# Block-sparse attention with a gated feed-forward layer: block numbers in one row, mask arithmetic on GpSimd, longer first K copies in the plan

## The chip, the cores and the metric

The kernel runs on one core of a Trainium2 chip. The metric is the device time of one execution in microseconds (us), given as the median of several runs. A core has TensorE (PE, with its weight loads shown as PEld), VectorE (DVE), ScalarE (ACT), GpSimd (POOL) and SyncE (SP); each takes its instructions in order, and they wait for each other through semaphores. Transfers are started by SP, ACT or POOL.

## What is computed

Attention over 4 batches, 8 heads, 768 positions of width 64, in blocks of 32 positions (24 blocks), and then a layer over the 3072 rows of 512 that come out. The mask lets a query block see its neighbours, the first and the last block, and three sampled blocks; the first and last query blocks see everything.

```python
scores = scale * np.matmul(q, k.transpose(0, 1, 3, 2))
mask = np.abs(blk_i - blk_j) <= window
mask = mask | (blk_i == 0) | (blk_j == 0) | (blk_i == n_blocks - 1) | (blk_j == n_blocks - 1)
for qb in range(n_blocks):
    for kb in sampled_blocks[qb]:
        mask[qb * block:(qb + 1) * block, kb * block:(kb + 1) * block] = True
attn = softmax(np.where(mask, scores, -1e9))
x = (attn @ v) as rows of 512
h = x @ w_in                                   # 512 -> 2048
out = (h / (1 + np.exp(-beta * h))) @ w_out    # 2048 -> 512
```

The block numbers `sampled_blocks` are 24 x 3 integers of 64 bits, known only at run time.

## The kernel before

Work is cut into tasks, each a short stretch of instructions of one engine. `add(name, engine, duration, emit, deps, prio, ...)` records a task with a planned duration. `Plan.run` (L51) then plays the tasks on the engines with those durations and priorities (smaller goes first), and its order is the order in which the instructions are written out. Where a task may run on two engines, the plan picks one by planned end times. So a changed planned duration changes the order on every engine and the engine of some tasks, and never the amount of work. `hw` and `dma` model a transfer, and `slack` delays a task after the tasks it depends on.

The attention goes by pairs of query blocks: 11 pairs in each of 4 batches, numbered n = 0 to 43. For each pair:

- `kg` (POOL, L560): reads six block numbers into registers and copies the six sampled K blocks from `KT` into a buffer `KG` (L566). `kn` (DVE or POOL, L569) adds the neighbour, first and last blocks.
- `sc` (PE, L653): first a matmul that writes the mask into the score bank (L658), then the scores from `KG` and `QT` (L668).
- `mx` (DVE, L679) row maxima, `ex` (ACT, L687) exponentials, `rc` (DVE, L693) reciprocals, `nrm` (POOL or DVE, L699) normalisation.
- `tp` (PE, L711) transposes, `ptv` (DVE, L715) their copy, `av` (PE, L727) the product with the gathered V blocks `VG`, `xv` (L735) its copy into `xT`.

`VG` comes by transfers from a V table in memory (SP, L627; tables written at L535), except the sampled V blocks of the first four pairs, which PE picks with 0/1 selection matrices (`pick`, L638). The first and last query blocks run as full rows (`gs` to `gx`, L754 to L827). The feed-forward layer runs in eight groups of rows: `h` (PE, L868), `tanh` (ACT, L874), `stt` (DVE, L879), `y` (PE, L896), output (ACT).

Ahead of all that stands the front, which the change touches:

- SP loads K, Q and V of batch 0 in halves of 768 KB (L433), ACT's queue loads the block numbers into `sbl` (`sbl`, L291: 72 single 4-byte words, the low halves of the 64-bit numbers) and then beta (L395).
- POOL turns the numbers into floats `sf` (L307) and into two tables of offsets (L309: `idx`), makes constants (`selc`, L364) and a half-precision row of block numbers (`srow`, L372).
- DVE computes the mask from `sf` in three tasks (`mask.0` to `mask.2`, L313 to L337): a sampled block that lies within the window, is the first or last block, or repeats an earlier one is masked out of its sampled place, since it is counted elsewhere. Each condition gives 0 or 1, joined by maximum, then scaled into a row `mrow`. PE spreads the row to 128 partitions (`maskb`, L342), DVE copies it into `maskr` (`maskc`, L345).
- PE makes the selection values from `srow` (`selb`, L379 and L381), ACT copies them (`selw`, L385), DVE compares them with the partition's position (`sel16`, L388).
- DVE casts K and Q of batch 0 to half precision (`cast`, L442), PE transposes them (`trK`, `trQ`, L508), ACT copies the transposes into `KT` and `QT` (`evK`, `evQ`, L259 and L265). DVE casts V (`vperm0`, L261).

The first gather needs `idx` and all four `evK`; the first `sc` needs `kg`, `kn`, `maskc` and all `evQ`.

Of the kernel before, what the change touches and what calls it, by code (L numbers as in the profile page):

```python
# [12 lines left out]
I32 = mybir.dt.int32  # L13
AF = mybir.ActivationFunctionType
ALU = mybir.AluOpType
# [3 lines left out]
NEG = -30000.0  # L19
# [16 lines left out]
class Plan:  # L36
# [9 lines left out]
    def add(self, *a, **k):  # L46
        t = Task(*a, **k)
        self.tasks.append(t)
        return t
# [133 lines left out]
def kernel(  # L183
# [11 lines left out]
    nc = tc.nc  # L195

    B, H, S, D = q.shape
    BLK = 32
    NB = S // BLK
# [15 lines left out]
    def sb(name, shape, dt=FP16):  # L215
        return pool.tile(shape, dt, name=name)
# [36 lines left out]
    add = plan.add  # L253
# [14 lines left out]
                out=out, in0=in_, scalar1=by, scalar2=1.0, op0=ALU.mult, op1=ALU.mult)  # L268


    sbl = sb("sbl", [1, NB, 3], I32)
    ctx_nc = nc

    def emit_ident():
# [2 lines left out]
    t_ident = add("ident", "POOL", 2.0, emit_ident, prio=-100)  # L277
# [3 lines left out]
    def emit_warm():  # L281
# [3 lines left out]
        out=warm[:, 0:1], in_=warm[:, 1:2], func=AF.Exp), deps=[t_warm0], prio=-150)  # L285

    def emit_sbl():
        src = sampled_blocks.tensor
        import dataclasses
        h = dataclasses.replace(src, shape=[NB, 6], dtype=I32)  # L290
        nc.scalar.dma_start(out=sbl, in_=bass.AP(tensor=h, offset=0, ap=[[0, 1], [6, NB], [2, 3]]))  # L291
    t_sbl = add("sbl", "ACT", 0.5, emit_sbl, prio=-200, dma=0.3, hw=1)

    sf = sb("sf", [1, NB - 2, 3], FP32)
    si = sb("si", [1, NB - 2, 3], FP32)
    sd = sb("sd", [1, NB - 2, 3], FP32)
    se = sb("se", [1, NB - 2, 3], FP32)
# [5 lines left out]
    t_iota = add("iota", "POOL", 0.6, emit_iota, prio=-99)  # L303

    def emit_idx():
        V = nc.gpsimd
        V.tensor_copy(out=sf, in_=sbl[:, 1:NB - 1, :])  # L307
        for t, m in ((offP, 16.0), (offV, 32.0)):
            V.tensor_scalar(out=t[:, :, 0:6], in0=sf[:, :, :].rearrange("o (p g) r -> o p (g r)", g=2),  # L309
                            scalar1=m, scalar2=1.0, op0=ALU.mult, op1=ALU.mult)  # L310
    t_idx = add("idx", "POOL", 0.6, emit_idx, deps=[t_sbl], prio=-99)

    def emit_mask0():  # L313
        V = nc.vector
        V.memset(sm5, 0.0)
        V.memset(sm5[:, 0:1, 3:4], 1.0)
        V.memset(sm5[:, NB - 3:NB - 2, 4:5], 1.0)
        V.tensor_tensor(out=sd, in0=sf, in1=si, op=ALU.subtract)
        V.tensor_tensor(out=sd, in0=sd, in1=sd, op=ALU.mult)
        V.tensor_scalar(out=sd, in0=sd, scalar1=1.5, scalar2=None, op0=ALU.is_lt)  # L320

    def emit_mask1():
        V = nc.vector
        V.tensor_scalar(out=se, in0=sf, scalar1=0.0, scalar2=None, op0=ALU.is_equal)
        V.tensor_tensor(out=sd, in0=sd, in1=se, op=ALU.max)
        V.tensor_scalar(out=se, in0=sf, scalar1=float(NB - 1), scalar2=None, op0=ALU.is_equal)
        V.tensor_tensor(out=sd, in0=sd, in1=se, op=ALU.max)
        V.tensor_tensor(out=se[:, :, 1:3], in0=sf[:, :, 1:3], in1=sf[:, :, 0:2], op=ALU.is_equal)

    def emit_mask2():  # L330
        V = nc.vector
        V.tensor_tensor(out=sd[:, :, 1:3], in0=sd[:, :, 1:3], in1=se[:, :, 1:3], op=ALU.max)
        V.tensor_tensor(out=se[:, :, 2:3], in0=sf[:, :, 2:3], in1=sf[:, :, 0:1], op=ALU.is_equal)
        V.tensor_tensor(out=sd[:, :, 2:3], in0=sd[:, :, 2:3], in1=se[:, :, 2:3], op=ALU.max)
        V.tensor_copy(out=sm5[:, :, 0:3], in_=sd)
        V.tensor_scalar(out=mrow, in0=sm5[:, :, :].rearrange("o a b -> o (a b)"),
                        scalar1=NEG / D, scalar2=None, op0=ALU.mult)  # L337
    t_mrow = None
    for part, f in enumerate((emit_mask0, emit_mask1, emit_mask2)):
        t_mrow = add(f"mask.{part}", "DVE", 0.95, f, deps=[t_idx, t_iota, t_ident, t_mrow], prio=-66.5)  # L340
    NM = (NB - 2) * 5
    t_mb = add("maskb", "PE", 0.3, lambda: nc.tensor.matmul(  # L342
        bank("mask")[:, 0:NM], lhsT=ones[0:1, :], rhs=mrow, start=True, stop=True),
        deps=[t_mrow], prio=-90, lat=0.2, opens=("mask",))
    t_mask = add("maskc", "DVE", 0.2, lambda: nc.vector.tensor_copy(  # L345
        out=maskr[:, :, :].rearrange("x a b -> x (a b)"), in_=bank("mask")[:, 0:NM]),
        deps=[t_mb], prio=-66, closes=("mask",))
# [16 lines left out]
    def emit_selc():  # L364
# [8 lines left out]
        out=srow, in_=sf[:, 0:2 * NSEL, :].rearrange("o a r -> o (a r)")), deps=[t_idx], prio=-98)  # L373
    t_selw = []
    for f in range(2):
        def emit_sb(f=f):
# [9 lines left out]
            out=sel16[:, f * SH:(f + 1) * SH], in_=bank(("selb", f))[:, 0:SH]),  # L386
            deps=[tb], prio=-88, closes=(("selb", f),)))
    t_sel = [add(f"sel16.{j}", "DVE", 0.27, lambda j=j: nc.vector.tensor_scalar(  # L388
        out=sel[j], in0=sel16, scalar1=pj[:, j:j + 1], scalar2=None, op0=ALU.is_equal),
        deps=t_selw, prio=-66.2) for j in range(J)]  # L390
# [5 lines left out]
        out=beta_row, in_=moe_beta.rearrange("(q x) -> q x", q=FQ)), prio=-140, dma=0.1, hw=1)  # L396
    t_id32 = add("id32", "DVE", 0.2, lambda: nc.vector.tensor_copy(
        out=ident32, in_=identity[0:4, 0:4]), deps=[t_ident], prio=-64)

    def emit_betaT():  # L400
        for i in range(4):
# [3 lines left out]
                  deps=[t_beta0, t_id32], prio=-55, lat=0.2, opens=("beta",))  # L405
    t_beta = add("betah", "DVE", 0.2, lambda: nc.vector.tensor_scalar(
        out=beta_sb[:, :].rearrange("x (q i) -> x i q", i=4),
        in0=bank("beta")[:, 0:N_FFC].rearrange("x (i q) -> x i q", i=4),
        scalar1=0.5, scalar2=None, op0=ALU.mult),
        deps=[t_betaT], prio=-55, closes=("beta",))  # L410
# [20 lines left out]
    for i, (nm, t, dst) in enumerate((("K", k, RK), ("Q", q, RQ), ("V", v, None))):  # L431
        for f in range(2):
            tl = add(f"ld{nm}0.{f}", "SP", 0.47, lambda i=i, t=t, f=f: nc.sync.dma_start(  # L433
                out=stage_half(i, f) if i < 2 else v_stage[:, f * HH:(f + 1) * HH, :],
                in_=src6(t, 0, f * HH, HH)), prio=-80 + i * 2 + f, dma=2.0, hw=1)
# [3 lines left out]
            for hp in range(2 * f, 2 * f + 2):  # L439
# [3 lines left out]
                        out=dst[:, 2 * hp:2 * hp + 2, :], in_=stage32(i, hp)),  # L443
                    deps=[tl], prio=-72 + 4 * i + hp)
# [13 lines left out]
    for c in range(4):  # L458
        for f in range(2):
            ps = slice(64 * f, 64 * f + 64)  # L460
            t_win.append(add(f"win{c}.{f}", "POOL", 0.6, lambda c=c, ps=ps: nc.gpsimd.dma_start(
                out=w_in_sb[ps, c, :], in_=w_in_r[c, ps, :]),
                deps=[tch], prio=-50 + 0.2 * c + 0.1 * f, dma=1.3, bulk=THR))
    for c in range(4):
        for f in range(2):
            ps = slice(64 * f, 64 * f + 64)
            t_wout.append(add(f"wout{c}.{f}", "POOL", 0.6, lambda c=c, ps=ps: nc.gpsimd.dma_start(
                out=w_out_sb[ps, 4 * c:4 * c + 4, :].rearrange("x i m -> x (i m)"), in_=w_out_r[c, ps, :]),
                deps=[tch], prio=-49 + 0.2 * c + 0.1 * f, dma=1.3, bulk=THR))
# [7 lines left out]
    for b in range(B):  # L477
        pr = prep_prio(b)
        if b:
            vperm[b] = []  # L480
            for nm, t, raw in (("V", v, RV), ("K", k, RK), ("Q", q, RQ)):
                tr = {"K": trK, "Q": trQ}.get(nm)
                for f in range(2):
# [4 lines left out]
                    else:  # L488
# [3 lines left out]
                             deps=free + [t_wout[-1]] if b == 1 else free,  # L492
                             prio=(-40 if b == 1 else pr - 30) + "VKQ".index(nm) + 0.5 * f, dma=2.55, bulk=THR)
# [8 lines left out]
        for nm, s16, dstT, tr, ev in (("K", RK, KT, trK, evK), ("Q", RQ, QT, trQ, evQ)):  # L502
            for hp in range(NHP):
                def emit_tr(nm=nm, s16=s16, b=b, hp=hp):
                    o = bank16((nm, b, hp))
                    for j in range(J):
                        for u in range(2):
# [5 lines left out]
                                prio=pr + hp, lat=0.2, opens=((nm, b, hp),))  # L513

                def emit_ev(eng, nm=nm, dstT=dstT, b=b, hp=hp):
# [4 lines left out]
                    else:  # L520
                        scale_on(eng, dst, src, SCALE)
                ev[b, hp] = add(f"ev{nm}{b}.{hp}", {"ACT": 0.71, "DVE": 0.86}, None, emit_ev,
                                deps=[tr[b, hp]], prio=pr + hp, closes=((nm, b, hp),))
# [3 lines left out]
        if b == 0:  # L527
            vperm[0], vtab[0] = [], []
            for f in range(2):
# [4 lines left out]
                    deps=[v0ld[f]], prio=-65))  # L534
                vtab[0].append(add(f"vtab0.{f}", "SP", 0.45, lambda cs=cs, vt_rows=vt_rows: nc.sync.dma_start(  # L535
                    out=vt_rows[:, :, cs], in_=Vn[0][:, :, cs]),
                    deps=[vperm[0][f]], prio=-64, dma=1.3, hw=1))
# [10 lines left out]
    for n, (b, p) in enumerate(order_pairs):  # L548
        pr = n * 10
# [37 lines left out]
                C(out=dst[:, 1, :, SN * w:(SN + 1) * w], in_=src[:, :, (NB - 1) * w:NB * w])  # L587
                C(out=dst[:, 1, :, (SN + 1) * w:(SN + 3) * w], in_=src[:, :, i0 * w:(i0 + 2) * w])
        kdeps = [evK[b, hp] for hp in range(NHP)] + ([sc[n - NKG]] if n >= NKG else [])
        kg[n] = add(f"kg{n}", "POOL", 1.15, emit_kg, deps=[t_idx] + kdeps, prio=pr)  # L590
        kn[n] = add(f"kn{n}", {"POOL": 0.5 + 0.6 * first_k, "DVE": 0.45 + 0.25 * first_k}, None,
                    emit_kn, deps=kdeps, prio=pr)

# [361 lines left out]
```

## Time and profile before

| what | value |
|---|---|
| three runs: median (range) | 316.14 us (315.14 to 317.6) |
| the profiled execution: time, span of its instructions | 316.81 us, 315.0 us |
| PE busy | 291.3 us, 92% of the span |
| DVE busy | 232.1 us, 74% |
| ACT busy | 212.4 us, 67% |
| POOL busy | 185.4 us, 59% |
| granted TensorE clock, mean | 0.978 |
| block numbers: issue on ACT's queue | 1.36 us from 0.74 |
| K of batch 0: first and second half landed | 4.8 us after an issue at 0.75; 6.8 us after one at 1.26 |
| first gather copy on POOL (L566) | 13.24 us |
| first pick on PE (L638) | 19.62 us |

All figures but the first line come from one profiled execution. Times in a timeline count from the start of the span. "Busy" is the time with an instruction in flight on an engine; an idle time is put down to the event that ended it. A PE that is busy need not be at its peak, since the granted clock can be lower and weight loads overlap.

### The profile page before, as it was taken

To read this page: it belongs to the slowest core of one execution; us is meant where nothing else is said; L and a number is where in the kernel's file an instruction comes from. 1 tells how busy PE (TensorE), PEld (TensorE's weight loads), DVE (VectorE), ACT (ScalarE), POOL (GpSimd) and SP (SyncE) were. 2 spreads that over 40 slices of the span, in tenths; PEclk is the share of its full clock that TensorE was granted. 3 is DMA by queue.
4 is the path that set the end of the run, shared out by engine and by line. 5 is a ranking of instruction groups with operands and counts; after the bars stand their busy time and mean duration, and the time that the engine had idled before them with its cause. 6 is when DMAs were issued, how large, how long until landed. Compare 5 with 4: busy or idle time off the path is not lost.

```text
span 315.0 us, 12633 instructions
## 1 busy us (share of the span) xinstructions
PE 291.3 (92%) x4569; PEld 179.8 (57%) x4569; DVE 232.1 (74%) x536; ACT 212.4 (67%) x625; POOL 185.4 (59%) x534
## 2 busy tenths in 40 slices
PE   0889869998989899999999999999999999999994
PEld 0645558756946676556556565545655555554671
DVE  2972785988899999999985478999679845670160
ACT  1753757875876989778785579857679835671361
POOL 3389985988388797599687354648836842200000
PEclk9999956999999999999999999999999999999999
DMA  7969999699976886345899752234233341100201
GB/s 248 354 138 209 218 212 194 125 202 248 204 152 133 250 151 137 109 129 100 151 171 242 175 152 77 67 115 109 83 90 90 84 138 49 35 1 33 100 2 67
DMA packets 41546, 43.70 MB, mean 139 GB/s; under 512 B 6152, under 2 KB 37000, under 8 KB 41484
## 3 DMA queue, kind: packets, MB, share of 16 engines
q1 hardware_dynamic: 27088, 25.32, 27.8%
q0 software_dynamic: 10784, 11.27, 24.1%
q10 hardware_dynamic: 3612, 6.30, 5.5%
q8 instruction: 36, 0.59, 0.8%
q14 instruction: 26, 0.21, 0.2%
HBM read 44.70 MB, written 9.44 MB: 172 GB/s over the span
## 4 chain that ended last, share of the span: by engine, by line
PE 68%; DMA 7%; DVE 7%; issue 5%; POOL 4%; SPq 3%; POOLq 1%; ACT 1%; DVEq 0%; ACTq 0%
PE bank L868 23%; PE bank L896 22%; PE bank L727 7%; PE bank L711 6%; DMA RQ<-in_q_dram 6%; PE bank L668 2%; SPq L627 2%; PE bank L658 2%; POOL KG L566 2%; PE bank L508 2%; DMA VG<-VT 1%; PE bank L638 1%; DVE SG L773 1%; POOLq L561 1%; DVE ST L679 1%
## 5 line engine op out<-in xcount | busy, mean ns | idle before, releaser
L699 POOL TENSOR_SCALAR PP<-PP,ST 128x256 f16<-128x256 f16 x176 | 83.5, 490 | 35.7 <-DVE ST L693 31.1
L868 PE MATMUL bank<-xT,w_in_sb 128*128 128x256 f16 (+1 forms) x512 | 94.9, 332 | 1.9 <-DVE g L879 1.3
L687 ACT ACTIVATE PP<-bank,ST 128x256 f16<-128x256 f32 x176 | 81.6, 485 | 17.5 <-DVE ST L679 14.3
L896 PE MATMUL bank<-w_out_sb,g 128*128 128x512 f16 x384 | 91.3, 380 | 0.8 <-DVE g L879 0.8
L874 ACT ACTIVATE t<-bank,beta_sb 128x512 f16<-128x512 f32 (+1 forms) x128 | 70.0, 595 | 18.6 <-PE bank L868 15.5
L879 DVE SCALAR_TENSOR_TENSOR g<-t,bank 128x512 f16<-128x512 f16 (+1 forms) x128 | 66.4, 547 | 19.6 <-ACT t L874 19.2
L566 POOL COPY KG<-KT 128x64 f32 x264 | 53.9, 253 | 34.1 <-PE bank L668 26.7
L868 PEld LDWEIGHTS <-w_in_sb 128*128 128x128 f16 x512 | 54.2, 115 | 26.5 <-issue 4.8
L679 DVE TENSOR_REDUCE ST<-bank 128x2 f32<-128x512 f32 x88 | 57.3, 680 | 10.7 <-PE bank L668 10.6
L896 PEld LDWEIGHTS <-g 128*128 128x128 f16 x384 | 34.7, 98 | 39.2 <-issue 4.5
L715 DVE COPY PT<-bank 128x1024 f16<-128x1024 f16 x44 | 30.2, 685 | 14.1 <-PE bank L711 13.6
L687 ACT ACTIVATION_READ_ACCUMULATOR PP<-bank,ST 128x1 f32 x176 | 38.2, 217 | 0.0
L727 PEld LDWEIGHTS <-VG 128*64 128x64 f16 x1408 | 27.4, 115 | 17.3 <-issue 13.1
L727 PE MATMUL bank<-PT,VG 128*64 128x32 f16 x1408 | 31.5, 186 | 4.3 <-issue 2.1
L265 ACT ACTIVATE osb<-bank 128x512 f32<-128x512 f32 x24 | 14.4, 599 | 22.8 <-PE bank L896 22.7
L711 PE MATMUL bank<-identity,PP 128*128 128x128 f16 x352 | 28.4, 225 | 0.5 <-DVE PTG L801 0.3
L711 PEld LDWEIGHTS <-PP 128*128 128x128 f16 x352 | 23.0, 100 | 7.6 <-POOL PP L699 0.9
L780 ACT ACTIVATE PG<-bank,SG 128x384 f16<-128x384 f32 x32 | 18.3, 578 | 5.2 <-DVE ST L693 2.3
L668 PE MATMUL bank<-KG,QT 64*32 64x256 f16 x704 | 18.8, 278 | 0.9 <-POOL KG L566 0.8
L791 POOL TENSOR_SCALAR PG<-PG,SG 128x768 f16<-128x768 f16 x14 | 13.2, 946 | 9.4 <-ACT PG L780 3.8
L259 ACT CAST xT<-bank 128x256 f16<-128x256 f32 x25 | 9.5, 381 | 12.8 <-PE bank L727 11.0
L773 DVE TENSOR_REDUCE SG<-bank 128x1 f32<-128x384 f32 x32 | 16.1, 546 | 0.6 <-PE bank L759 0.5
(94 smaller groups left out, 261.7 us busy)
## 6 DMA issues: line engine op xcount, KB each, us to landing
VG<-VT SPq DMA_DIRECT2D x244, 32.0 KB, 2.8
VG<-VT SPq DMA_DIRECT2D x40, 192.0 KB, 3.8
out_dram<-osb ACTq DMA_DIRECT2D x20, 256.0 KB, 2.2
RV<-in_v_dram POOLq DMA_DIRECT2D x6, 384.0 KB, 5.8
RK<-in_k_dram POOLq DMA_DIRECT2D x6, 384.0 KB, 6.3
RQ<-in_q_dram POOLq DMA_DIRECT2D x6, 384.0 KB, 6.0
VT<-Vn SPq DMA_DIRECT2D x3, 768.0 KB, 6.0
w_in_sb<-in_moe_w_in_dram POOLq DMA_DIRECT2D x8, 256.0 KB, 8.0
```

Source lines behind the costliest of these rows:

```text
L566: nc.gpsimd.tensor_copy(out=kg32[:, g, :, (SR + r) * W:(SR + r + 1) * W], in_=kt32[:, :, bass.ds(vals[3 * g + r], W)])
L668: nc.tensor.matmul(bk[u][hp * BLK:(hp + 1) * BLK, g * 256:(g + 1) * 256], lhsT=QT[b % 2][u * D:(u + 1) * D, hp, (i0 + g) * BLK:(i0 + g + 1 ...
L679: mx[n, u] = add(f"mx{n}.{u}", "DVE", 0.6, lambda n=n, u=u, sb_=sb_: nc.vector.tensor_reduce(out=sb_[:, 0, 2 * u:2 * u + 2], in_=bank(("S" ...
L687: nc.scalar.activation(out=pb[:, u, g, :], in_=bank(("S", n, u))[:, g * 256:(g + 1) * 256], func=AF.Exp, bias=sb_[:, 0, 2 * u + g:2 * u + ...
L699: (nc.vector if eng == "DVE" else nc.gpsimd).tensor_scalar(out=pb[:, u, g, :], in0=pb[:, u, g, :], scalar1=sb_[:, 2, 2 * u + g:2 * u + g + ...
L711: nc.tensor.transpose(out=o[:, s * P:(s + 1) * P], in_=pb[:, u, g, c * P:(c + 1) * P], identity=identity)
L715: ptv[n] = add(f"ptv{n}", "DVE", 0.61, lambda n=n: nc.vector.tensor_copy(out=PT[n % NPT], in_=bank16(("T", n))), deps=[tp[n]] + ([av[n - N ...
L727: nc.tensor.matmul(o[us, (g * NHP + hp) * BLK:(g * NHP + hp + 1) * BLK], lhsT=vgb[:, g, c, (2 * hp + u) * D:(2 * hp + u + 1) * D], rhs=pt[ ...
L868: nc.tensor.matmul(o[:, 0:TW], lhsT=w_in_v[:, c, f // 4, f % 4, :], rhs=xT[:, c, c0:c0 + TW], start=(c == 0), stop=(c == NHP - 1))
L874: lambda G=G, f=f, TW=TW, tt=tt: nc.scalar.activation(out=tt[:, 0:TW], in_=bank(("H", G, f))[:, 0:TW], func=AF.Tanh, bias=0.0, scale=beta_ ...
L879: lambda G=G, f=f, TW=TW, tt=tt, gg=gg: nc.vector.scalar_tensor_tensor(out=gg[:, f, 0:TW], in0=tt[:, 0:TW], scalar=1.0, in1=bank(("H", G, ...
L896: nc.tensor.matmul(o[:, :], lhsT=gg[:, f, s * P:(s + 1) * P], rhs=w_out_sb[:, f, :], start=(f == 0), stop=(f == N_FFC - 1))
```

## The change

Three edits. The block numbers are loaded whole, as one contiguous row of 144 words (`sbl` grows from 3 to 6 words per block), and the conversion to `sf` takes every second word. The mask tasks move from DVE to POOL: `mask.0` now holds only the three memsets and depends on nothing, `mask.1` and `mask.2` compute the conditions and join them by addition in place of maximum (a masked place then holds a count of 1 or more), with an equality between two rows written as a subtraction and a comparison with zero; they get priorities (-98.8, -97, -96) that put them before the first gather. The plan's duration of the gathers of pairs 0, 1 and 2 rises from 1.15 to 2.6, 2.6 and 1.6. The `slack` on `sbl` stands on a task that depends on none.

```diff
-    sbl = sb("sbl", [1, NB, 3], I32)
+    sbl = sb("sbl", [1, NB, 6], I32)
...
-        nc.scalar.dma_start(out=sbl, in_=bass.AP(tensor=h, offset=0, ap=[[0, 1], [6, NB], [2, 3]]))
-    t_sbl = add("sbl", "ACT", 0.5, emit_sbl, prio=-200, dma=0.3, hw=1)
+        nc.scalar.dma_start(out=sbl, in_=bass.AP(tensor=h, offset=0, ap=[[0, 1], [6, NB], [1, 6]]))
+    t_sbl = add("sbl", "ACT", 0.5, emit_sbl, prio=-200, dma=0.3, hw=1, slack=0.8)
...
-        V.tensor_copy(out=sf, in_=sbl[:, 1:NB - 1, :])
+        V.tensor_copy(out=sf, in_=sbl[:, 1:NB - 1, 0::2])
...
     def emit_mask0():
-        V = nc.vector
+        V = nc.gpsimd
         V.memset(sm5, 0.0)
         V.memset(sm5[:, 0:1, 3:4], 1.0)
         V.memset(sm5[:, NB - 3:NB - 2, 4:5], 1.0)
+
+    def emit_mask1():
+
+        V = nc.gpsimd
         V.tensor_tensor(out=sd, in0=sf, in1=si, op=ALU.subtract)
         V.tensor_tensor(out=sd, in0=sd, in1=sd, op=ALU.mult)
         V.tensor_scalar(out=sd, in0=sd, scalar1=1.5, scalar2=None, op0=ALU.is_lt)
-
-    def emit_mask1():
-        V = nc.vector
-        V.tensor_scalar(out=se, in0=sf, scalar1=0.0, scalar2=None, op0=ALU.is_equal)
-        V.tensor_tensor(out=sd, in0=sd, in1=se, op=ALU.max)
-        V.tensor_scalar(out=se, in0=sf, scalar1=float(NB - 1), scalar2=None, op0=ALU.is_equal)
-        V.tensor_tensor(out=sd, in0=sd, in1=se, op=ALU.max)
-        V.tensor_tensor(out=se[:, :, 1:3], in0=sf[:, :, 1:3], in1=sf[:, :, 0:2], op=ALU.is_equal)
+        for to in (0.0, float(NB - 1)):
+            V.tensor_scalar(out=se, in0=sf, scalar1=to, scalar2=None, op0=ALU.is_equal)
+            V.tensor_tensor(out=sd, in0=sd, in1=se, op=ALU.add)
 
     def emit_mask2():
-        V = nc.vector
-        V.tensor_tensor(out=sd[:, :, 1:3], in0=sd[:, :, 1:3], in1=se[:, :, 1:3], op=ALU.max)
-        V.tensor_tensor(out=se[:, :, 2:3], in0=sf[:, :, 2:3], in1=sf[:, :, 0:1], op=ALU.is_equal)
-        V.tensor_tensor(out=sd[:, :, 2:3], in0=sd[:, :, 2:3], in1=se[:, :, 2:3], op=ALU.max)
+        V = nc.gpsimd
+        for far in (1, 2):
+            V.tensor_tensor(out=se[:, :, far:3], in0=sf[:, :, far:3], in1=sf[:, :, 0:3 - far], op=ALU.subtract)
+            V.tensor_scalar(out=se[:, :, far:3], in0=se[:, :, far:3], scalar1=0.0, scalar2=None, op0=ALU.is_equal)
+            V.tensor_tensor(out=sd[:, :, far:3], in0=sd[:, :, far:3], in1=se[:, :, far:3], op=ALU.add)
         V.tensor_copy(out=sm5[:, :, 0:3], in_=sd)
         V.tensor_scalar(out=mrow, in0=sm5[:, :, :].rearrange("o a b -> o (a b)"),
-                        scalar1=NEG / D, scalar2=None, op0=ALU.mult)
-    t_mrow = None
-    for part, f in enumerate((emit_mask0, emit_mask1, emit_mask2)):
-        t_mrow = add(f"mask.{part}", "DVE", 0.95, f, deps=[t_idx, t_iota, t_ident, t_mrow], prio=-66.5)
+                        scalar1=NEG / D, scalar2=1.0, op0=ALU.mult, op1=ALU.mult)
+    t_m0 = add("mask.0", "POOL", 0.4, emit_mask0, prio=-98.8)
+    t_m1 = add("mask.1", "POOL", 0.9, emit_mask1, deps=[t_idx, t_iota], prio=-97)
+    t_mrow = add("mask.2", "POOL", 1.0, emit_mask2, deps=[t_m1, t_m0], prio=-96)
...
-        kg[n] = add(f"kg{n}", "POOL", 1.15, emit_kg, deps=[t_idx] + kdeps, prio=pr)
+        kg[n] = add(f"kg{n}", "POOL", 2.6 if n < 2 else 1.6 if n == 2 else 1.15, emit_kg, deps=[t_idx] + kdeps, prio=pr)
```

In the built program the front's order becomes: on POOL `idx`, `mask.0`, `selc`, `srow`, `mask.1`, `mask.2`, `kg0`, `kg1`; on DVE four K casts, three `sel16`, two Q casts, three `sel16`, `maskc`, two Q casts; on PE `trK0.0`, `selb0`, `selb1`, `trK0.1`, `maskb`, `trK0.2`, `trK0.3`; on ACT `evK0.0`, `selw0`, `selw1`, `evK0.1`. Before, `selb0`, `selb1` and `selw0`, `selw1` came first, and the mask tasks stood on DVE before the first cast and between the second and third.

## The prediction

> **What bounds the kernel now.** I read the page first, then busy time by stage, then the first 20 us instruction by instruction, because everything the diff edits lies there. By stage (stage, its length, busy time of PE, PEld, DVE, ACT, POOL, then granted clock, DMA share, GB/s):
>
> ```profile
> span 315.0 us, 12633 instructions
> PE 291.3 (92%) x4569; PEld 179.8 (57%) x4569; DVE 232.1 (74%) x536; ACT 212.4 (67%) x625; POOL 185.4 (59%) x534
> ...
> 0.00:19.60 19.60, 9.79 (x153) 6.99 (x153) 13.06 (x44) 8.92 (x15) 8.85 (x30) 1.00 0.78 262
> 19.60:36.60 17.00, 16.94 (x204) 9.26 (x196) 8.52 (x20) 8.86 (x32) 15.56 (x47) 1.00 1.07 202
> 36.60:52.40 15.80, 11.73 (x208) 9.01 (x207) 10.66 (x28) 10.30 (x42) 12.36 (x28) 0.57 1.05 213
> 52.40:80.00 27.60, 26.16 (x531) 19.05 (x531) 23.94 (x64) 20.86 (x66) 22.92 (x67) 1.00 0.94 189
> 80.00:120.00 40.00, 37.33 (x774) 28.11 (x770) 37.98 (x92) 33.56 (x102) 28.77 (x77) 1.00 0.83 178
> ```
>
> See that PE has no slack from 19.6 to 36.6 us (16.94 of 17.00): whatever moves the start of that stage moves all of it. PE is idle 9.8 us before it, 4.1 us in the next stage, 1.4 and 2.7 us in the two after. So the change is worth what it does to the moment when PE's first long run (the picks, L638) starts, plus what a new order does to 8.2 us of later idle time.
>
> The timeline of the front (start, length, instruction; in brackets the idle time before it and what ended it):
>
> ```profile
> 6.06 0.23 POOL L307 CAST sf<-sbl 1x66 f32<-1x66 int32 x1 [4.22 <-DMA sbl<-in_sampled_blocks_dram]
> ...
> 6.39 0.27 POOL L309 TENSOR_SCALAR offP<-sf 1x66 int32<-1x66 f32 x1
> ...
> 6.74 0.24 POOL L309 TENSOR_SCALAR offV<-sf 1x66 int32<-1x66 f32 x1
> ...
> 8.06 1.01 DVE L442 CAST RK<-g 128x768 f16<-128x768 f32 x2
> ...
> 10.59 0.27 PE L342 MATMUL bank<-mrow,ones 1*128 1x110 f16 x1
> 10.79 1.25 PEld L508 LDWEIGHTS <-RK 128*64 128x64 f16 x24
> ...
> 13.24 5.98 POOL L566 COPY KG<-KT 128x64 f32 x12 [5.49 <-ACT KT L259]
> ...
> 15.51 0.94 DVE L261 CAST Vn<-xT 128x1536 f16<-128x1536 f32 x1
> ```
>
> Block numbers reach POOL at 6.06. DVE then does mask arithmetic and casts the first K half only at 8.06, though that half landed 4.8 us after its issue at 0.75, so at 5.55 (next lines; the second K half at 8.05, the first Q half at 10.2). K's transposes, their copies on ACT and the first gather copies (13.24) follow from that.
>
> ```profile
> g<-in_k_dram SPq DMA_DIRECT2D x1, 768.0 KB, 4.8
> ...
> g<-in_k_dram SPq DMA_DIRECT2D x1, 768.0 KB, 6.8
> g<-in_q_dram SPq DMA_DIRECT2D x1, 768.0 KB, 8.4
> ```
>
> The line view of the gather copies, between 13 and 19.2 us, gives least, median and greatest duration in ns:
>
> ```profile
> L566 POOL COPY KG<-KT x12: 227/232/2580, 13.2 to 19.0; 128x64 f32 x12
> ```
>
> A copy of 0.23 us took 2.58 us. Its neighbours show when: it spans from 13.97 to 16.55, and DVE's Vn cast ends at 15.51 + 0.94 = 16.45. All that time DVE ran SBUF copies and casts back to back (two RQ casts, three KG copies, the Vn cast), and POOL did not get in between any two of them.
>
> **Part 1, the contiguous row.** Its issue took 1.36 us on ACT and POOL got the data at 6.06, after the first K half (5.55). The nearest short issue is beta's, 0.31 us; K's own first issue took 0.46. Bounds: POOL starts at about 2.9 if the row leaves before K's packets (an estimate: the DMA share is 0.07 up to 2 us and 0.93 from 2 to 4), or 5.5 if it still queues behind that half. I take 2.9, as a 0.31 us issue that starts with K's (0.74 and 0.75) ends first.
>
> **Part 2, the mask on POOL.** Removed from DVE: 13 small operations between 6.33 and 10.08, about 2.9 us, so the K casts can begin at 5.55. Added to POOL ahead of the first gather: 3 memsets and 15 operations on one partition, all but one dependent on the one before. A dependent pair on POOL starts 0.33 to 0.35 us apart (6.06, 6.39, 6.74); I take 0.35.
> - Row at 2.9; conversions, memsets, constants and the row's half copy start to start as now (1.5) plus 0.35 for the memsets plus 0.2: mask.1 starts at about 5.0. Two operations are through at 5.6.
> - DVE casts the first K half, 5.55 to 6.6 (1.01 us as at 8.06). Then POOL finishes mask.1, five operations, 1.6 us: 8.2.
> - At 8.05 the second K half lands. In the built order DVE now has, without a wait that lasts: two K casts (to 9.1), three selection compares of 0.33 (to 10.1; their input is ready at 8.9: one K transpose group of 0.75 from 6.1, then the 1.95 us that now lie between the first selection matmul and the end of the second ACT copy), two Q casts (to 11.2), three compares (to 12.3), then the mask's copy-out, which waits for PE. If POOL stays out as at 13.97, the eight operations of mask.2 run from 12.3 to 15.1 (8 x 0.35).
> - PE is in order, and the mask matmul (L342 before) stands between the second and third K transposes. Before it ran at 10.59 with no cost, and 2.65 us later the gathers began (13.24). Now it runs at 15.2, the gathers begin at 17.85: **4.6 us later**.
> - Part comes back. ACT's four Q copies (0.75 each) end at 20.8, the first score group follows then (16.86 before, +3.9); gathers of pairs 0 and 1 need 12 x 0.18 + 0.95 behind one Vn cast + 0.6 behind KG copies, so 21.5; second score group to 22.6; DVE's second Vn cast, behind beta and the third KG set, ends at 22.8. The picks start at 22.8, not 19.62: **+3.2 us**, carried through the busy stage.
>
> Bounds of this price: if POOL is never shut out, mask.2 ends at 10.0, the gathers start at 12.7 (-0.5); if it loses one DVE instruction per operation, eight times 0.55 from 8.1, it ends at 12.5, gathers at 15.1 (+1.9), picks +1.0. I take full exclusion because the rows nearest to it (same casts, same compares: another copy took 0.78 us beside the last compares at 13.24) show exclusion.
>
> The Trainium skill weighs in here: "SBUF — State Buffer", section "Who interferes with whom", says that copies, casts and tensor_scalar can take a port pair shared with GpSimd, as an exclusive lock for one whole instruction, issue order deciding who blocks. By that rule a waiting POOL operation loses one DVE instruction, about the +1.0 case; the 2.58 us row lost six. The same skill's "GPSIMD Engine Reference", section "Performance versus the Vector engine", puts a two-input operation at 1.96 times DVE's; with DVE's 0.22 us row for 66 elements that would add an estimated 0.16 us (0.43 less the 0.27 of a POOL row) to each of mask.2's four, 0.6 us and so 320.2 for the sum, which no run here shows.
>
> **Part 3, order and queues.** The longer planned copies put nrm0 after three gathers and not after five, which POOL reached at 27.55 though its input stood at 23.3; but PE was busy with picks till 28.6 and waited 0.3 us, so I count nothing. w_in's issues shift with the gathers by about 2.5 us; the last was issued at 33.75 and lands in some 8 us, and the first matmul that reads it is at 47.65: hidden by 5.9 us. SP's V-table writes wait for the Vn casts (second: 17.44, now 21.8, +4.4), and its V loads queue behind them; the first matmul reading those had waited 0.2 us for them, so up to 1.2 us beyond the 3.2 may show. I keep that for the range. ACT's selection copies now stand behind one K copy: inside the wait above. From group 4's last up-projections on, about 200 us, PE's order is the same as now; before that, tasks are shuffled, with one nrm and net three KG copies moved from POOL to DVE. PE's idle time bounds what that can gain (8.2 us) and I see no row that gives it a sign: 0, with 3 either way for the range.
>
> **Sum.** +3.2. The profiled execution took 316.81 (span 315.0 plus 1.8 around it), 0.7 above the median of the three runs shown, 316.14; the four average 316.4. 316.4 + 3.2 = 319.6, 1.1% over the median.
>
> **Rivals.**
> - *Faster.* POOL's one-partition operations slip between DVE's instructions and the row is early, so the mask is done before the compares start (the deciding point: mask row before 10.2). For: they need the port for little of their 0.23 us, and from 16.8 to 17.5 copies of both engines did interleave. Against: the two rows above. Gathers 0.5 earlier, and the better POOL order takes some 3 of the 4.1 us idle in the stage to 52.4: 312.9.
> - *Hidden.* Alternation, +1.0 at the picks, or the 3.2 partly made up in the 8.2 us of idle: 317.4.
> - *Worse.* The row still queues behind the first K half, so POOL starts at 5.5: conversions and the selection row are then themselves shut out, compares move to about 11.7 and mask.2 to some 18: picks +5.5, 321.9. For: beta's four packets, issued by 2.5, ran only from 6.1 to 7.3 by the trace. Against: the shorter issue.
>
> **How the numbers follow.** The forecast gets 0.36, faster 0.22, hidden 0.29, worse 0.13. One per cent, about what a measurement of this kernel can tell from no change, is 3.2 us: bounds 313.0 and 319.3. Faster 0.22, same 0.29, slower 0.36 + 0.13 = 0.49. The range 313.0 to 323.5 cuts half of the faster case and the end of the worse. The likeliest case's own range is 317.6 to 321.8: from +1.2 (a new order worth 2) to +5.4 (1.2 more for the V tables and an order that costs 1).
>
> **What would show it.** Right: block row read by POOL near 3 us; K casts from 5.6; a gap or a stretched operation on POOL between 8 and 12 beside DVE's compares and Q casts; the mask matmul near 15 with PE and ACT idle before it; gathers from about 17.9, picks from 22.8. Wrong: mask operations at a steady 0.35 through DVE's casts, gathers before 14, picks before 20.5, or a stage from 36 to 120 us whose PE idle time changes by more than 3 us.

## The result, and the profile after

The changed kernel took 320.9 us (median of 13 runs, 318.77 to 327.0) against 317.95 for the kernel before (13 runs beside it, 315.14 to 321.25). The ratio is 1.0111, 95% interval 1.0076 to 1.0146: about 1.1% slower. The profiled execution took 320.02, with a span of 318.1. The forecast was 319.6, slower by 1.1%. So the total came out as forecast; the sum behind it did not.

Ratios here leave out runs that lie over 1.5% above the fastest of their kernel; for two of the experiments (the longer K copies alone, and the second splice) that is more than half of their 12 runs, so for those the medians of all runs are told and the ratio is not relied on.

The head of the page after:

```profile
span 318.1 us, 12630 instructions
...
PE 288.2 (91%) x4569; PEld 177.7 (56%) x4569; DVE 235.0 (74%) x529; ACT 210.5 (66%) x623; POOL 189.0 (59%) x545
```

The span is 3.1 longer. PE was busy 3.1 less, so it was idle 6.2 more: 318.1 - 288.2 = 29.9 against 315.0 - 291.3 = 23.7. Most of the fall in busy time lies in the picks (L638), the same 48 matmuls in both: 15.9 us before and 13.1 after. PE's timeline of some of them (start, length), first before, then after:

```profile
19.62 1.94 PE L638 MATMUL bank<-Vn,xT 128*96 128x512 f16 x4
21.35 1.06 PE L638 MATMUL bank<-Vn,sel 128*96 128x512 f16 x2
22.20 1.91 PE L638 MATMUL bank<-Vn,xT 128*96 128x512 f16 x4
```

```profile
20.66 1.03 PE L638 MATMUL bank<-Vn,xT 128*96 128x512 f16 x4
21.52 0.59 PE L638 MATMUL bank<-Vn,sel 128*96 128x512 f16 x2
21.95 1.03 PE L638 MATMUL bank<-Vn,xT 128*96 128x512 f16 x4
```

From one group of six to the next it is 2.58 us before and 1.29 after. The first 13 picks before took 567 to 660 ns each and the later ones about 379; after, none took more than 417. So PE before ran at half rate up to about 25 us, though the column of the granted clock reads 1.00 there: the trace holds no clock record before 25.1 us (before) and 17.2 (after), and the column counts that time as full. (Where a record says half clock, as at 28 to 31 us in the row and POOL mask in the old order, below, a pick takes the same 634 ns.) The changed kernel's execution thus had an advantage of 2.8 us in the picks, which its span does not show: it was lost again later. Whether the earlier full rate comes with the change, or only fell so in these two executions, is not shown. The half clock that is recorded later, between 37 and 53 us, lasted 13.7 us before and 10.2 after.

Left to place are the 6.2 us of PE idle time. By stage, with the columns as before (start and end, length, busy time of PE, PEld, DVE, ACT, POOL, granted clock, DMA share, GB/s), first after:

```profile
0.00:19.60 19.60, 9.36 (x155) 6.86 (x156) 11.40 (x31) 8.51 (x13) 14.30 (x48) 1.00 0.75 259
19.60:36.60 17.00, 15.35 (x232) 9.14 (x231) 9.84 (x21) 10.62 (x39) 15.88 (x47) 1.00 1.05 217
36.60:52.40 15.80, 11.78 (x266) 9.23 (x265) 12.48 (x36) 10.17 (x40) 11.98 (x35) 0.68 1.08 221
52.40:80.00 27.60, 25.26 (x478) 18.82 (x462) 22.46 (x59) 19.41 (x64) 19.12 (x49) 1.00 0.95 193
80.00:120.00 40.00, 35.69 (x678) 25.41 (x672) 36.90 (x86) 31.87 (x98) 29.41 (x84) 1.00 0.83 175
...
120.00:145.00 25.00, 23.50 (x543) 14.54 (x543) 23.87 (x63) 20.99 (x76) 21.99 (x63) 1.00 0.47 115
145.00:190.00 45.00, 43.46 (x690) 24.39 (x696) 35.28 (x70) 29.94 (x84) 26.31 (x74) 1.00 0.69 157
```

and before, the two stages that were not shown:

```profile
120.00:145.00 25.00, 23.81 (x442) 13.68 (x437) 23.45 (x61) 21.34 (x76) 20.41 (x60) 1.00 0.43 120
145.00:190.00 45.00, 44.81 (x792) 26.52 (x792) 34.29 (x65) 31.42 (x86) 29.57 (x91) 1.00 0.77 168
```

Length less PE busy, after against before: 10.24 for 9.81 in the front, 1.65 for 0.06, 4.02 for 4.07, 2.34 for 1.44, 4.31 for 2.67, 1.50 for 1.19, 1.54 for 0.19. The front, the one stage whose instructions the change edits, adds 0.4 of the 6.2. The rest is spread from 20 to 190 us, over stages in which only the order and the engine of some tasks differ. In the stage from 19.6 to 36.6 the faster picks may have a part in it: the last one ends at 32.79 and not at 34.67, and PE comes sooner to work whose inputs are not there yet. From group 4's up-projections on, at about 185 us, the distance stays between 3.0 and 3.2.

The timeline of the front after (start, length, engine, line; in brackets the idle time before it and what ended it):

```profile
0.75 0.53 ACTq L291 DMA_DIRECT2D sbl<-in_sampled_blocks_dram  x1
...
2.04 0.23 POOL L307 CAST sf<-sbl 1x66 f32<-1x66 int32 x1 [0.18 <-DMA sbl<-in_sampled_blocks_dram]
...
5.55 1.16 DVE L442 CAST RK<-g 128x768 f16<-128x768 f32 x2 [4.04 <-DMA g<-in_k_dram]
...
5.59 0.70 POOL L327 TENSOR_TENSOR sd<-sd,se 1x66 f32<-1x66 f32 x1
...
7.75 1.09 POOL L333 TENSOR_SCALAR se<-se 1x44 f32<-1x44 f32 x1
8.93 0.28 POOL L334 TENSOR_TENSOR sd<-sd,se 1x44 f32<-1x44 f32 x1
9.29 0.24 POOL L332 TENSOR_TENSOR se<-sf 1x22 f32<-1x22 f32 x1
9.62 1.49 POOL L333 TENSOR_SCALAR se<-se 1x22 f32<-1x22 f32 x1
...
10.03 1.02 DVE L442 CAST RQ<-g 128x768 f16<-128x768 f32 x2
...
12.23 0.25 PE L342 MATMUL bank<-mrow,ones 1*128 1x110 f16 x1 [3.05 <-POOL mrow L336]
...
14.87 0.47 POOL L566 COPY KG<-KT 128x64 f32 x2 [2.69 <-ACT KT L259]
...
19.33 0.85 PE L638 MATMUL bank<-Vn,xT 128*96 128x512 f16 x3
```

Read it in three steps. The row lands early (read at 2.04, before 6.06), and the K casts begin at 5.55. The mask's operations on POOL are then held up four times beside a DVE cast (0.70, 0.56, 1.09 and 1.49 us, while the other operations on `sd` and `se` take 0.24 to 0.39), so the mask matmul comes at 12.23 and not at 15.2 as forecast (before 10.59). And the gathers, though 1.6 us later (14.87 for 13.24), are done sooner, because the Q casts now lie ahead of them; in the line view of the twelve copies no copy takes 2.58 us any more:

```profile
L566 POOL COPY KG<-KT x12: 232/304/964, 14.9 to 18.8; 128x64 f32 x12
```

So the picks start at 19.33, not later than before (19.62). The 3.2 us that the forecast put at the picks are not there.

### The profile page after: what moved, and what is told of

It reads as the page before. It is cut to its first block, busy times and chain, and to the rows that moved or that the text cites. A ratio compares the mean times of both kernels' runs of the same rounds, so it can differ in the third digit from the quotient of the medians.

```text
span 318.1 us, 12630 instructions
## 1 busy us (share of the span) xinstructions
PE 288.2 (91%) x4569; PEld 177.7 (56%) x4569; DVE 235.0 (74%) x529; ACT 210.5 (66%) x623; POOL 189.0 (59%) x545
## 4 chain that ended last, share of the span: by engine, by line
PE 62%; DVE 15%; DMA 6%; issue 5%; POOL 3%; ACT 2%; SPq 2%; POOLq 1%; DVEq 0%; ACTq 0%
PE bank L896 23%; PE bank L868 17%; PE bank L727 6%; PE bank L711 5%; DVE g L879 4%; DVE ST L679 3%; DMA RQ<-in_q_dram 3%; DMA RK<-in_k_dram 2%; PE bank L668 2%; PE bank L638 2%; DVE PT L715 2%; PE bank L658 2%; PE bank L508 2%; DVE SG L773 2%; POOL KG L566 1%
## 5 line engine op out<-in xcount | busy, mean ns | idle before, releaser
L879 DVE SCALAR_TENSOR_TENSOR g<-t,bank 128x512 f16<-128x512 f16 (+1 forms) x128 | 66.6, 545 | 19.3 <-ACT t L874 19.0
L566 POOL COPY KG<-KT 128x64 f32 x264 | 52.9, 249 | 33.3 <-PE bank L668 23.9
L715 DVE COPY PT<-bank 128x1024 f16<-128x1024 f16 x44 | 29.9, 684 | 14.8 <-PE bank L711 14.2
L727 PE MATMUL bank<-PT,VG 128*64 128x32 f16 x1408 | 30.8, 185 | 5.7 <-DVE PT L715 3.1
L711 PE MATMUL bank<-identity,PP 128*128 128x128 f16 x352 | 29.1, 226 | 1.5 <-DVE PTG L801 1.0
L261 DVE COPY KG<-KT 128x768 f16<-128x768 f16 (+3 forms) x51 | 17.0, 375 | 1.2 <-ACT KT L259 1.1
```

What stands on the lines that cost most here:

```text
L566: nc.gpsimd.tensor_copy(out=kg32[:, g, :, (SR + r) * W:(SR + r + 1) * W], in_=kt32[:, :, bass.ds(vals[3 * g + r], W)])
L711: nc.tensor.transpose(out=o[:, s * P:(s + 1) * P], in_=pb[:, u, g, c * P:(c + 1) * P], identity=identity)
L715: ptv[n] = add(f"ptv{n}", "DVE", 0.61, lambda n=n: nc.vector.tensor_copy(out=PT[n % NPT], in_=bank16(("T", n))), deps=[tp[n]] + ([av[n - N ...
L727: nc.tensor.matmul(o[us, (g * NHP + hp) * BLK:(g * NHP + hp + 1) * BLK], lhsT=vgb[:, g, c, (2 * hp + u) * D:(2 * hp + u + 1) * D], rhs=pt[ ...
L879: lambda G=G, f=f, TW=TW, tt=tt, gg=gg: nc.vector.scalar_tensor_tensor(out=gg[:, f, 0:TW], in0=tt[:, 0:TW], scalar=1.0, in1=bank(("H", G, ...
```

## The experiments

Each version was timed beside the kernel before on the same chip, in five rounds. Two orders of tasks come up again and again: the *old order* (the plan of before) and the *new order* (the plan of the changed kernel). Of 428 tasks on PE 89 change place between them, and 38 tasks other than the mask's change engine.

| version | median | before | ratio (95%) |
|---|---|---|---|
| contiguous row alone, old order | 317.37 | 316.15 | 1.0000 (0.9957 to 1.0044) |
| row and POOL mask, old order | 315.12 | 316.15 | 0.9965 (0.9926 to 1.0004) |
| row, mask on DVE, new order | 319.17 | 316.15 | 1.0086 (1.0048 to 1.0124) |
| longer planned K copies alone | 318.25 | 316.15 | 0.9994 (0.9942 to 1.0046), five of 12 runs |
| changed kernel without the longer K copies | 320.08 | 316.32 | 1.0105 (1.0055 to 1.0154) |
| before, plan's delay 0.19 for 0.18 | 318.95 | 316.32 | 1.0083 (1.0048 to 1.0119) |
| before, plan's delay 0.17 for 0.18 | 320.31 | 316.32 | 1.0101 (1.0053 to 1.0148) |
| changed kernel, four loads earlier | 320.34 | 316.55 | 1.0087 (1.0044 to 1.0130) |
| row and POOL mask, old order, four loads earlier | 317.26 | 316.32 | 1.0040 (1.0011 to 1.0070) |
| new order on the old engines | 322.95 | 316.55 | 1.0162 (1.0095 to 1.0229) |
| new order to task 600, then old | 325.84 | 316.55 | 1.0306 (1.0232 to 1.0380) |
| old order to task 600, then new | 319.49 | 316.55 | 0.9956 (0.9882 to 1.0031), three of 12 runs |

### The front in the old order, and the order with the old mask

The first three take the change apart: the instructions of the front in the old order, and the new order with the mask's instructions where they were.

The row alone:

```diff
-    sbl = sb("sbl", [1, NB, 3], I32)
+    sbl = sb("sbl", [1, NB, 6], I32)
...
-        nc.scalar.dma_start(out=sbl, in_=bass.AP(tensor=h, offset=0, ap=[[0, 1], [6, NB], [2, 3]]))
+        nc.scalar.dma_start(out=sbl, in_=bass.AP(tensor=h, offset=0, ap=[[0, 1], [6, NB], [1, 6]]))
...
-        V.tensor_copy(out=sf, in_=sbl[:, 1:NB - 1, :])
+        V.tensor_copy(out=sf, in_=sbl[:, 1:NB - 1, 0::2])
```

> The kernel before with nothing but the contiguous block row; its plan gives the same order and the same engines as before. Three readings of the loss of 1.1% are weighed in this call. ORDER (mine now): the front of the changed kernel costs nothing net (its picks start at 19.33, before at 19.62) and the loss arises between about 119 and 186 us from the new order and engine choice of the plan. FRONT (the forecast on record): POOL's mask is shut out beside VectorE's casts and the late gathers are carried to the end. KDUR (a part of ORDER): the longer planned K copies alone make the new order. Here all three expect a gain at the front: DVE's mask done by about 8 instead of 10.1, the mask matmul near 8.5 instead of 10.59, gathers from about 11.5 instead of 13.24. ORDER: carried only in part, since later PE idle time absorbs it: 0 to 2 us faster, 316 to 318 against 317.9. FRONT: carried in full, about 2 us faster.

Measured: no difference (ratio 1.0000), though the front is faster by as much as expected: first gather copy at 10.83, picks at 17.13, 2.5 us earlier than before. By stage in this version:

```profile
0.00:19.60 19.60, 12.24 (x165) 8.47 (x166) 14.90 (x47) 10.36 (x21) 10.91 (x39) 1.00 0.83 269
19.60:36.60 17.00, 13.30 (x222) 7.85 (x220) 9.40 (x21) 9.88 (x36) 15.15 (x46) 1.00 1.06 225
...
80.00:120.00 40.00, 35.26 (x715) 25.15 (x716) 35.67 (x85) 31.23 (x98) 27.29 (x73) 0.96 0.82 173
```

PE gains 2.4 us of idle time in the front (7.36 for 9.81) and is idle 3.7 in the next stage, which had no slack before (0.06): with the picks ahead of the rest it waits for gathered V, reciprocals and normalised rows. (All its picks ran at the full rate, 376 to 417 ns, so the last one ended at 30.97, 3.7 us earlier than before.) It gains 2.0 back between 36.6 and 80, and then is idle 4.74 from 80 to 120 (before 2.67) and runs 3.4 us at half clock there. A lead from the front is eaten by later stages whose inputs come at their own pace. That falls outside what FRONT expected (2 us faster) and at the edge of what ORDER did.

Row and POOL mask in the old order: the mask tasks stay in the plan as DVE tasks of 0.95 us with their old dependences, and only their instructions go to POOL, with sums.

```diff
     def emit_mask0():
-        V = nc.vector
+        V = nc.gpsimd
...
     t_mrow = None
     for part, f in enumerate((emit_mask0, emit_mask1, emit_mask2)):
         t_mrow = add(f"mask.{part}", "DVE", 0.95, f, deps=[t_idx, t_iota, t_ident, t_mrow], prio=-66.5)
```

> The kernel before, its order and engine choice kept by planning the mask tasks as they were (as VectorE tasks with the old durations), but with the contiguous row and the mask's instructions issued on POOL with sums. So the front of the change without its new order. ORDER: mask matmul near 12, picks near 19 to 20, total within 1 us of before (317 to 319). FRONT: as the changed kernel, +3 us (about 321) with the picks at 22.

Measured: 1.0 us faster in the median, ratio 0.9965 with 1 just inside its interval; picks at 17.93. POOL's mask costs nothing here. FRONT, which wanted 3 us slower, falls.

The new order with the mask on DVE: the changed kernel with the mask tasks planned as POOL tasks, but with their instructions issued on DVE, with maxima.

```diff
-        V = nc.gpsimd
+        V = nc.vector
...
-        for to in (0.0, float(NB - 1)):
-            V.tensor_scalar(out=se, in0=sf, scalar1=to, scalar2=None, op0=ALU.is_equal)
-            V.tensor_tensor(out=sd, in0=sd, in1=se, op=ALU.add)
+        V.tensor_scalar(out=se, in0=sf, scalar1=0.0, scalar2=None, op0=ALU.is_equal)
+        V.tensor_tensor(out=sd, in0=sd, in1=se, op=ALU.max)
```

> The changed kernel's order and engine choice kept (mask tasks planned as POOL tasks with the new durations, longer planned K copies), but the mask's instructions issued on VectorE with maxima as before. So the new order without POOL's mask. ORDER: the loss stays: output of group 4's gate up at 186 us as in the changed kernel against 183.3 before, total +2 to +3.5 (320 to 321.5). FRONT: no exclusion, so gathers near 11.5 and a total at or below before, 315 to 318.

Measured: 0.9% slower. The last stage in which the orders differ, first in the old order with the POOL mask, then in the new order with the DVE mask:

```profile
145.00:190.00 45.00, 45.00 (x769) 26.20 (x762) 34.36 (x62) 31.29 (x87) 27.63 (x87) 1.00 0.77 170
```

```profile
145.00:190.00 45.00, 43.81 (x701) 24.64 (x700) 35.16 (x70) 29.94 (x84) 25.99 (x75) 1.00 0.70 158
```

PE has no idle time in the one and 1.19 us in the other (the changed kernel 1.54). By the times, the loss goes with the order and not with the engine of the mask. The stage shows only 1.2 of the 4.5 us between these two traces (spans 312.9 and 317.4). Over the whole span their PE idle time is nearly the same, 26.1 and 26.4 us, and PE was busy 286.8 and 291.0; in the slower one the first 11 picks, up to 24.5 us, ran at the half rate seen above. So this pair does not show by which waits an order loses. The two parts do not add up to the whole exactly: -0.35% and +0.9% make +0.5%, the changed kernel has +1.1%; the intervals are wide enough for that.

### Which edit made the order

In the kernel before:

```diff
-        kg[n] = add(f"kg{n}", "POOL", 1.15, emit_kg, deps=[t_idx] + kdeps, prio=pr)
+        kg[n] = add(f"kg{n}", "POOL", 2.6 if n < 2 else 1.6 if n == 2 else 1.15, emit_kg, deps=[t_idx] + kdeps, prio=pr)
```

> The kernel before with only the planned durations of the first three K copies raised (2.6, 2.6 and 1.6 us for 1.15); no instruction of the front changes, old row, VectorE mask. Its order differs from both. KDUR: most of the loss shows here, +2 to +3.5 us. ORDER with the loss from the moved mask tasks, or any reshuffle: within 1.5 us either way of before. FRONT: within 1 us of before, since nothing of the front's instructions moved.

Measured: the median of its 12 runs is 2.1 us above before, the ratio of the five that remain 0.9994. Unclear.

The reverse edit in the changed kernel:

```diff
-        kg[n] = add(f"kg{n}", "POOL", 2.6 if n < 2 else 1.6 if n == 2 else 1.15, emit_kg, deps=[t_idx] + kdeps, prio=pr)
+        kg[n] = add(f"kg{n}", "POOL", 1.15, emit_kg, deps=[t_idx] + kdeps, prio=pr)
```

> The changed kernel without the longer planned K copies: row, POOL mask, and the mask planned as POOL tasks. Of the 428 tasks on PE 86 change place against before (in the changed kernel 89), and 46 tasks change engine (38). RESHUFFLE: this is one more order that the plan makes from nearly the same durations, with no tie to the changed kernel's; such orders come out some 0 to 3 us slower than the one of before. KCOPY: the longer planned copies made the bad order; without them it is as the new front in the old order, 1 us faster than before.

Measured: 1.05% slower, as the changed kernel, so KCOPY falls: the longer copies are not needed for the loss. Two different edits of the plan gave two different orders with the same loss, which suggested that it takes no particular edit.

### Orders with no edit at all

The control: one constant of the plan, which no instruction depends on.

```diff
-    HOP = 0.18
+    HOP = 0.19
```

> The kernel before with one constant of its plan, the delay from one engine to the next, at 0.19 us for 0.18: no instruction is added, removed or changed, but 89 of the 428 PE tasks change place and 41 tasks change engine, as much as under the change. RESHUFFLE: slower than before by 1 to 3 us, since the order of before is one of the better ones. SPECIFIC: the changed kernel's order is bad for a reason of its own, and other orders come out within 1 us of before, to either side.

> The same with 0.17: 86 PE tasks change place, 36 tasks change engine. RESHUFFLE: 1 to 3 us slower than before. SPECIFIC: within 1 us of before, to either side.

Measured: 0.8% and 1.0% slower, medians 2.6 and 4.0 us above before. The same stage, first for 0.19, then for 0.17:

```profile
145.00:190.00 45.00, 44.00 (x736) 25.24 (x734) 36.12 (x65) 30.53 (x88) 27.58 (x82) 1.00 0.72 163
```

```profile
145.00:190.00 45.00, 44.02 (x757) 25.61 (x758) 37.20 (x74) 31.92 (x93) 28.82 (x80) 1.00 0.77 167
```

PE is idle 1.0 us in it in both (before 0.19), though no instruction of the front differs from before (picks at 19.93 and 19.64). These two traces are no measure of the loss itself: the one for 0.19 is the fastest of its 12 runs (315.11, span 313.4, shorter than before's 315.0), the one for 0.17 the slowest of its 6 (321.78, span 320.0). The loss is shown by the many runs of the table. By them RESHUFFLE holds (0.17 at or past the upper end of its 1 to 3 us), and SPECIFIC falls: moving as many tasks as the change moves, for no reason, costs about as much as the change. None of the other orders tried came out faster than the old one beyond its interval.

### Where in the order

In the changed kernel PE's longest waits between 104 and 121 us are for loads, by the view of waits (line, what was waited for, us in total, times, longest):

```profile
PE bank L508 <- DMA RK<-in_k_dram: 1.5, 1, 1.5
PE bank L508 <- DMA RQ<-in_q_dram: 1.0, 1, 1.0
```

They are the third batch's K and Q, issued on POOL's queue between its gathers and normalisations. The next version writes the four loads earlier:

```diff
     order = plan.run()
+    for name, at_ in (('ldK2.0', 505), ('ldK2.1', 540), ('ldQ2.0', 570), ('ldQ2.1', 600)):
+        i = [t.name for t in order].index(name)
+        order.insert(at_, order.pop(i))
```

> The changed kernel with only the four loads of the third K and Q moved ahead in the written order (tasks 548, 607, 627 and 660 to places 505, 540, 570 and 600, all on POOL's queue, issued some 5 to 9 us earlier). LOADS: the 2.5 us that PE waits for them at 110 to 115 go and are carried to the end: 1.5 to 2.5 us faster than the changed kernel, so 0.5 to 1.5 us slower than before. ABSORBED: PE reaches the stretch of 125 to 165 us earlier, where VectorE is busy 4.9 of every 5 us, and waits there instead: within 0.7 us of the changed kernel, so about 3 slower than before.

Measured: 0.9% slower, against 1.1%, as ABSORBED expected. The waits for loads between 104 and 121 us are gone, and one of 0.6 us is left:

```profile
PE bank L727 <- DVE PT L715: 0.6, 1, 0.6
```

From 120 to 190 us PE is idle 4.40 (23.09 busy of 25, 42.51 of 45) instead of 3.04, and in the profiled execution 17.1 us went at half clock instead of 10.2. The same edit in the row-and-POOL-mask version:

> The new front in the old order (the version that came out 1 us faster than before), with the four loads of the third K and Q moved ahead to places 505 to 600 of the written order. PE waits 1.8 us at 108 to 120 there. ABSORBED: those waits go, as they did in the changed kernel, and come back later or as time at half clock: within 1 us of that version, so 0 to 2 us faster than before. LOADS: 1.5 us faster than it, 2.5 faster than before.

Measured: 0.4% slower than before, so 0.75% worse than the same version with the loads in place, by two ratios from different chips. Neither expectation holds, since both had it faster than before. Closing the largest wait gave nothing in the one order and lost in the other.

Then the engines alone, in the changed kernel (the list of 38 cut here):

```diff
     order = plan.run()
+    for t in order:
+        t.eng = {'kn3': 'POOL', 'kn5': 'POOL', 'xv2': 'ACT',
...
+                 'kn35': 'DVE'}.get(t.name, t.eng)
```

> The changed kernel in its own order, but the 38 tasks that the plan gave to other engines (8 K gathers onto VectorE, four Q evictions onto VectorE, and so on) back on the engines of before. ENGINES: VectorE has less to do between 120 and 165 us, PE's 3.0 us of waits there fall to about 1.5: 1 to 2 us faster than the changed kernel. SEQUENCE: it is the order that does it, and with the old engines the order fits no better: within 1 us of the changed kernel, or slower.

Measured: 1.6% slower. The gain that ENGINES expected from relieving DVE does not show, and SEQUENCE holds. That an order and the engines chosen with it belong together would explain it, but was not tried by itself.

Last, two orders joined from both plans at task 600: the first 600 names of one plan and then, in the other plan's order, all that are left. `SPLICE` is that list written out, and PSUM banks are given out anew along it.

```diff
     order = plan.run()
+    todo = [(n[:-1], {"A": "ACT", "D": "DVE", "G": "POOL", "P": "PE", "S": "SP"}[n[-1]]) for n in SPLICE.split()]
...
+        t.eng = e
+        order.append(t)
...
+        for b_ in t.opens:
+            plan.bank[b_] = free_banks.pop(0)
```

> The changed kernel with the first 600 of its 1736 tasks in its own order (to about 95 us), the rest in the order, and on the engines, that the kernel before had for them. Two places are weighed, since the moved order is now the suspect. MIDDLE: the loss arises between 95 and 170 us (PE waits 2.5 us at 110 to 115 for loads of the third K and Q, and 3.0 us in all between 120 and 170, before 0.5 and 1.4); the early part is ahead of before by about 2 us at the third group's up-projections. Then this version is 0.5 to 2 us faster than before. EARLY: the early order is at fault (PE's idle time to 80 us is 18.3 against 15.4) and the rest only passes it on: 2 to 3 us slower than before.

> The reverse: the changed instructions (contiguous row, POOL mask), the first 600 tasks in the order of the kernel before, the rest in the order of the changed kernel. MIDDLE: the loss is there, 2 to 4 us slower than before. EARLY: within 1 us of before, or faster.

Measured: 3.1% slower, and a median 2.9 us above before with a ratio that rests on three runs. Neither expectation of the first holds, and the seam has a large part in it: full rows of two query blocks, which the new order puts after task 600 and the old one before it, fall late, and PE waits 3.9 us for one normalisation, up to 113.4 us, with 10.2 us at half clock around it (the view of waits of that version, 104 to 121 us):

```profile
PE bank L799 <- POOL PG L791: 4.2, 2, 3.9
```

So the splices do not say in which half the loss arises. The stage table of the changed kernel says that it is spread; which of the moved tasks matter stays open.

## Why the prediction came out right, and where it was wrong

- **Row at 2.9, K casts at 5.55.** Right: 2.04 and 5.55. The issue took 0.53, not the 1.36 of the scattered words.
- **POOL fully shut out from 8.1 to 12.3, mask.2 ending at 15.1.** This is the step that failed. It ended at 12.18, which is the forecast's middle bound (12.5). Eight operations took 4.8 us where 2.8 was the price without hindrance; two of them lost 0.8 and 1.2 us beside pairs of casts, and five ran at 0.24 to 0.29 beside the half-precision compares of L388. The "nearest row", the 2.58 us copy, had stood beside casts and copies alone. I had read it as what back-to-back DVE work does, where it showed what those casts and copies do. The other row I leaned on, 0.78 us beside the last compares, was a copy on 128 partitions, and the mask's operations on one partition did not follow it.
- **Gathers +4.6, picks +3.2.** Gathers +1.6, picks -0.3. That part of the loss comes back at the gathers was right in kind (their copies took 4.2 us for 6.0), and as large as the loss.
- **Carried to the end, since PE has no slack from 19.6 to 36.6.** Not so for a gain: picks 2.5 us earlier (the row alone) were worth nothing at the end, since a lead meets the next input. And the 16.94 busy of 17.00 us were not full in the sense meant: 13 of the 48 picks in them ran at half rate, which the clock column did not show. Whether a delay would have been carried was not tried, as no version here had its picks start more than 0.8 us late.
- **Order: 0, with 3 either way, for want of a row that gives it a sign.** The second failed step, and by the times the whole of the loss: +0.9% in the new order without POOL's mask, +0.8% and +1.0% in two orders without any edit. Rows did bear on the sign. PE idled 0.2 of 45 us and 1.2 of 25 in stages of before; an order that fills stages so far has little to win in them by a shuffle, and much to lose. That is an argument and no proof; of the five orders that were drawn anew, four came out 0.8 to 1.1% slower and one (the longer K copies alone) stays undecided.
- **The total.** +3.2 was forecast, and 1.1% measured: an error of about +3.5 at the picks and one of the same size, the other way, at the order. That they cancelled is chance, and the agreement is no support for the sum.
- **The port lock and the price of small operations.** On the exclusive lock for a whole instruction (the Trainium skill, "SBUF — State Buffer", section "Who interferes with whom"): the operations of 0.70 and 0.56 us each ended some 0.2 us after one cast had ended, which agrees; those of 1.09 and 1.49 us ended only after two casts of some 0.55 each, which the one-instruction reading does not give. On the factor of 1.96 (the Trainium skill, "GPSIMD Engine Reference", section "Performance versus the Vector engine"): two-input operations on 66 elements took 0.29 to 0.32 us here where DVE's took 0.22, and not the 0.43 that the estimate made of it.

## What to carry to other kernels

Where a planner writes the order, every change of a planned duration or engine draws a new order of the whole kernel; cost it as such, and look at PE's idle time stage by stage as a hint whether a draw has more to lose than to win. Before you call a stage full, compare the duration of one kind of matmul early and late in it: a busy PE at half rate looks full, and the clock column can miss it. Take the edit apart on the chip with the order held: the new instructions in the old order, the old instructions in the new order, and a control that moves a planning constant and nothing else. And a forecast that meets the measured total is not thereby explained: the milestones that it named (mask matmul, gathers, picks) showed within one trace that this one had the wrong cause.

## What had not been expected of the hardware

- The contiguous 576 bytes reached POOL at 2.04 us after an issue of 0.53; the same numbers as 72 words of 4 bytes reached it at 6.06 after an issue of 1.36.
- Small one-partition operations on POOL ran beside half-precision compares on DVE at their free price (0.24 to 0.29 us), and were held beside casts from full to half precision (0.56 to 1.49 us).
- PE ran at half rate at first, and the traces differ in when that ended: before, a pick took 660 ns at 19.6 us and 379 from 25.2 on; after, picks took about 379 from the first on, at 19.3. The clock records begin only at that change, at 25.1 and 17.2 us (at 12.7 and 25.0 with the plan's delay at 0.19 and 0.17, whose front has the same instructions as before), and the clock column reads 1.00 ahead of them.
- Time at half clock that is recorded differs between traces in steps of 3.4 us: 6.8 (POOL mask in the old order), 10.2 (after), 13.7 (before, and the row alone, there with one step as late as 116 us). As six picks take 2.58 us at half rate and 1.29 at full, one step costs a busy PE about 1.7 us, half of what the change cost, so a single trace does not decide between versions this close.
